# A transformer block with adaptive layer norm: the order of TensorE's products in the last row block's tail

## The chip, the cores and the metric

The kernel runs on one core of a Trainium2 chip. The metric is the device time of one execution in microseconds (us); the median of three runs is given.

## What is computed

The inputs are x (2048 rows of 576), weights for 32 heads of 18, a feed-forward layer of 4608, and a condition c. All is float32.

```python
mod = (_silu(c) @ w_mod).reshape(c.shape[0], 6, 1, -1)
sa, ca, ga, sb, cb, gb = (mod[:, i] for i in range(6))
h = _layernorm(x, axis=-1) * (1 + ca) + sa
x = x + ga * _A_ref(h, A_wqkv, A_wo)      # softmax attention, 32 heads, then @ wo
h = _layernorm(x, axis=-1) * (1 + cb) + sb
x = x + gb * _B_ref(h, B_w1, B_w2)        # silu(h @ w1) @ w2
```

## The kernel before, in words

The 2048 rows are worked on in four row blocks b = 0 to 3 of 512 rows, each of four tiles j of 128 rows. Every factor of a product outside attention is split into a high and a low float32r part, and a product is done as three (high x high, high x low, low x high); PASS lists these for the five contraction tiles kt, 14 steps in all (kt 4 has 64 rows and carries its low part in the other 64).

While attention of block b runs, the program fills TensorE's free slots with work of block b - 1. ORDER is the hand-written order of that mix; a planner (Plan, Filler) keeps dates for it. TensorE's order is the order in which the program emits its instructions; the order of ACT, DVE, GpSimd and of SyncE's DMA queue is found by a scheduler, which issues what is ready in its own simulated time. When attention of block 3 is over, `post(3)` runs with `last` true, and everything left is emitted in one row: the tail. Its stages, in TensorE's order, with lines:

1. Left work of block 2, the last second-layer group (weight tiles 32 to 35): a list `left` of 32 items, each of 3 products of 128x288. An item belongs to a row tile j and a half g of the 576 columns; `mlp2` (L1251) makes 12 products per bank, two banks per j. When a j is done, two adds (`add_x1`, L1103) put it on x1[j], and L1268 sends x1[j] out. `rest(n)` takes the next n items; REST = (16, 8, 0, 0) takes 16 before projection 0 and 8 before projection 1, and the last eight come after projection 3, two ahead of each step of its layer norm.
2. Out-projection `proj(j)` (L1084): 28 products of 128x288 for each j, 14 per bank. It needs the attention output as th and tl, made by `o_T` (L1077 to L1082) from the tile ou, which the last head group's DMAs (L1014) fill. Its adds need x1[j] of block 3, loaded by `prefetch(3)` at L1052. There are five x1 buffers for all blocks (`bufs=5`), and four tiles per block.
3. Layer norm of tile j (`ln_stat`, `ln_rs`, `ln_c`, L1112 to L1137), on DVE with one power on GpSimd; for j = 0 to 2 beside the next projection. The result is ob.
4. `h_T(kt)` (L1141): for each kt four transposes (one per j) into one bank, then ACT scales the bank into eq (`mod_out`, L472), DVE rounds eq to hh (`mod_hi`, L478), and DVE or GpSimd takes hl = eq - hh (`mod_lo`, L482, L484).
5. First layer `mlp1(i)` (L1218): a pair of weight tiles, 14 products of 128x512 for the first bank, then 14 for the second; then SiLU on ACT and DVE (L1244 to L1248) gives g tiles. Second layer as in 1, in groups of four g tiles, each group behind the next first-layer pairs; only the last group follows its own pair at once. w1 loads (L739, four buffers, which the wo tiles have before) and w2 loads (five buffers) wait for the products that free a buffer.

In a pair of banks the steps run 0 to 2n - 1, the first n for the first bank (class Pair, L531). `bank` (L1209) chooses the PSUM banks: psA has three, psF and psB two each, psV one. In the tail the first layer uses psA; second layer and transposes use psF and psB in turn, but block 2's left work only psF.

Of the kernel before, what the change touches and what calls it, by code (L numbers as in the profile page):

```python
# [9 lines left out]
F32 = mybir.dt.float32  # L10
# [8 lines left out]
P = 128  # L19
# [6 lines left out]
KT = 5  # L26
# [30 lines left out]
END = -4  # L57
END0 = 40
LP0 = 1000
REST = (16, 8, 0, 0)  # L60
LP = 8000
PB = 9
ORDER = (
# [43 lines left out]
GR = [[range(i, min(i + GS, n)) for i in range(0, n, GS)] for n in (28, 27)]  # L107
NG = len(GR[0])
GQ = (range(0, 5), range(5, 10), range(10, 14))
G2 = [range(i, i + 3) for i in range(0, 24, 3)]  # L110
GP = [range(i, i + 2) for i in range(0, 28, 2)]
MMC = 228
MMH = 131

# [292 lines left out]
def tile_adaln_block(ctx: ExitStack, tc: tile.TileContext, x, wqkv, wo, w1, w2, c, ccol, wfirst, wcol, out):  # L407
# [63 lines left out]
    def mod_out(ps, kt, which, tmp):  # L471
        nc.scalar.activation(tmp, ps, AF.Identity, scale=modc[:, 2 * which + 1, kt:kt + 1], bias=modc[:, 2 * which, kt:kt + 1])  # L472

    def mod_hi_ps(kt, hi_dst, ps):
        nc.vector.tensor_scalar(hi_dst, ps, modc[:, 1, kt:kt + 1], modc[:, 0, kt:kt + 1], op0=ALU.mult, op1=ALU.add)

    def mod_hi(hi_dst, tmp):
        nc.vector.tensor_copy(hi_dst, tmp)  # L478
# [52 lines left out]
    class Pair:  # L531
# [3 lines left out]

        def __init__(self, ps, ops, n, halves, planned=True, short=False):
            self.ps, self.ops, self.n, self.halves, self.planned = ps, ops, n, halves, planned
            self.end = 2 * n - 1 - (halves and short)  # L540
            self.both = halves and short
            if planned:
                self.release = [plan.take("f") for _ in ps]

        def step(self, s):
            late, i = divmod(s, self.n)
            if not self.halves:
                lhsT, rhs = self.ops(late, i)
                mm(self.ps[late], lhsT=lhsT, rhs=rhs, start=(i == 0), stop=(i == self.n - 1))  # L549
                return  # L550
            for h in (1, 0) if late else (0, 1):
                g = 1 - h if late else h
                lhsT, rhs = self.ops(g, self.n if self.both and s == self.n - 1 else i)
                rows = slice(64 * h, 64 * h + 64)
                done = mm(self.ps[g], lhsT=lhsT[rows], rhs=rhs[rows], start=(s == 0), stop=(s == self.end))  # L555
                if h == 1 and s == self.n - 1:
                    self.last = done
                    if self.planned:
                        self.change()
                        half["at"] = None  # L560
                        plan.op("A", plan.t + 200, 20, lambda t: half.update(at=t + TR))
                elif h == 1 and s == self.n:
                    tc.add_manual_dep(done.ins, self.turn.ins.name, SYNC, reason="the other halves' writes to this bank")
# [490 lines left out]
    def post(b):  # L1054
# [29 lines left out]
        def proj(j, part):  # L1084
            if part == 0:
                def ops(g, i):
                    kt, a, w = PASS[i]
                    return (c["tl"] if a else c["th"])[:, kt, j * P:(j + 1) * P], c["wo", kt][:, 1 - w, g * HH:(g + 1) * HH]

                settle(*[("wo", kt) for kt in range(KT)])  # L1090
                c["pp"] = Pair([bank("psp", psA)[:, :HH] for _ in range(2)], ops, 14, not state["tail"])
            for s in GP[part]:
                c["pp"].step(s)
            if part == len(GP) - 1:
                state["ln"] = b == 0
                c["x", j] = Event(plan)
                for g in range(2):
                    add_x1(j, g, c["pp"].ps[g], c["pp"].release[g], c["x", j].set)
# [39 lines left out]
        def ln_steps(j):  # L1138
            return [lambda: ln_stat(j, 0), lambda: ln_stat(j, 1), lambda: ln_rs(j), lambda: ln_c(j)]

        def h_T(kt):  # L1141
            if kt == 0:
                c["hh"] = pool.tile([P, KT, QB], F32R, tag="th", name="hh")
                c["hl"] = pool.tile([P, 4, QB], F32R, tag="tl", name="hl")
            ps = bank("psT", psF)
            c["hT", kt] = None
            chain([("A", 780), ("V", 800), ("G", 1290 if kt < 4 else 1900)], plan.t, plan.take("f"), lambda at: c.update({("hT", kt): at + 100}))
            for j in range(NST):
                nc.tensor.transpose(ps[:, j * P:(j + 1) * P], c["ob"][:, j, kt * P:(kt + 1) * P], ident)
            tmp, hi = etmp(), c["hh"][:, kt, :]  # L1150
            mod_out(ps, kt, 1, tmp)
            mod_hi(hi, tmp)
            if kt == 4 and not last:
                c["h2"] = const.tile([P, D], F32R, tag="ga", name="h2")[:, :QB]
                nc.gpsimd.tensor_copy(c["h2"], tmp)
            mod_lo(kt, hi, c["hl"][:, kt, :] if kt < 4 else None, tmp, nc.vector if last and kt % 2 == 0 else nc.gpsimd)

        def rest(n):
            for _ in range(min(n, len(left))):
                fl.add(*left.pop(0))  # L1160
# [7 lines left out]
            return all_ready(pair_need(), *[c.get(("th_at", kt)) for kt in range(KT)], weights_need(*[("wo", kt) for kt in range(KT)]) if b == 0 else 0)  # L1168

        for j in range(NST):  # L1170
            rest(REST[j])
            steps_ = dict(zip((1, 4, 8, 11), ln_steps(j - 1))) if j else {}
            for part in range(len(GP)):
                fl.add(MMH * len(GP[part]), lambda j=j, part=part: proj(j, part), need={0: pair_need if j else o_need, len(GP) // 2: half_need}.get(part))
                if b == 0 and j == 0 and part in (1, 4, 7, 10):
                    fl.add(0, lambda i=part // 3: w2_load(i))
                if part in steps_:
                    fl.add(0, steps_[part])
        for step in ln_steps(3):
# [1 line left out]
                fl.add(700)  # L1181
            rest(2)
            fl.add(0, step)
        rest(99)
        if b == 0 and not EARLY:
            fl.add(LP)

# [21 lines left out]
        def bank(name, pool_):  # L1209
            if last and pool_ is psA:  # L1210
                return psA.tile([P, 512], F32, tag="a", name=name)
            if last and state["tail2"]:
                state["tail2"] = False
                return psB.tile([P, 512], F32, tag="b", name=name, bufs=2)
            state["tail2"] = True
            return psF.tile([P, 512], F32, tag="f", name=name)

        def mlp1(i, part):  # L1218
            if part == 0:
                def ops(g, k):  # L1220
                    if k == 14:
                        return c["w1", i + g][:, 0, 4 * P:], c["h2"]
                    kt, a, w = PASS[k]
                    return c["w1", i + g][:, 1 - w, kt * P:(kt + 1) * P], (c["hl"] if a else c["hh"])[:, kt, :]

                settle(("w1", i), ("w1", i + 1))
                c["p1"] = Pair([bank("ps1", psA) for _ in range(2)], ops, 14, not state["tail"], short=not last)
            for s in GR[not last][part]:
                c["p1"].step(s)
            if part < NG - 1:  # L1230
# [17 lines left out]
                (nc.vector if last else nc.gpsimd).tensor_tensor(g[:, 1, :], t, f(g[:, 0, :]), op=ALU.subtract)  # L1248
                c["g", i + g_] = g

        def mlp2(i0, j, part):  # L1251
            if part == 0:
                def ops(g, n):
                    a, w = ((0, 0), (0, 1), (1, 0))[n % 3]
                    return c["g", i0 + n // 3][:, a, j * P:(j + 1) * P], c["w2", i0 + n // 3][:, 1 - w, g * HH:(g + 1) * HH]

                settle(*[("w2", i0 + n) for n in range(CH)])
                c["p2"] = Pair([bank("ps2", psF)[:, :HH] for _ in range(2)], ops, 3 * CH, not state["tail"])
            for s in G2[part]:
                c["p2"].step(s)  # L1260
            if part < len(G2) - 1:
                return
            if j == NST - 1:
                c["freed"] = i0 + 2 * CH - 1
            for hf in range(2):
                add_x1(j, hf, c["p2"].ps[hf], None if state["tail"] else c["p2"].release[hf])
            if i0 + CH == NFT:
                nc.sync.dma_start(out[b * QB + j * P:b * QB + (j + 1) * P, :], c["x1"][j])  # L1268

# [7 lines left out]
            fl.add(0, lambda i=i: w_load(i))  # L1277
        if b:
            fl.add(0, lambda: w2_load(0))
        if EARLY:  # L1280
            if b == 0:
                fl.add(LP)
            for kt in range(KT):
                fl.add(440, lambda kt=kt: h_T(kt), name=["h_T"], need=hT_need, mode="full")
                if b == 0 and kt > 2:
                    fl.add(0, lambda i=kt - 1: w_load(i))
# [14 lines left out]
                fl.add(MMC * len(GR[not last][part]), lambda part=part: mlp1(i, part), need={0: first_need, NG // 2: half_need}.get(part))  # L1301
                w_at(part, *loads)

        def add_mlp2(i0, add, *loads):
            def first_need():
                return all_ready(pair_need(), weights_need(*[("w2", i0 + n) for n in range(CH)]) if b == 0 else 0)

            for j in range(NST):
                for part in range(len(G2)):
                    add(MMH * len(G2[part]), lambda j=j, part=part: mlp2(i0, j, part), None, {0: first_need, len(G2) // 2: half_need}.get(part))  # L1310
                    w_at(j * len(G2) + part, *loads)

        add_mlp1(0, *([] if b else [(9, w_load, 4), (11, w_load, 5)]))
        for i0 in range(0, NFT, CH):
# [9 lines left out]
            else:  # L1324
                add_mlp1(i0 + 2, *([(0, w2_load, i0 + 1), (2, w2_load, i0 + 2), (4, w2_load, i0 + 3)] if b else []))
        if last:
            add_mlp2(NFT - CH, fl.add)
        else:
            fl.add(0, lambda: prefetch(b + 1))
            add_mlp2(NFT - CH, lambda *a: left.append(a))  # L1330

            def left_need():
                return all_ready(pair_need(), *c["gs"], weights_need(*[("w2", NFT - CH + n) for n in range(CH)])) if len(c["gs"]) == 2 else None
# [509 lines left out]
```

## Time and profile before

| | us |
|---|---|
| median of three runs (2340.99 to 2346.88) | 2342.13 |
| the profiled execution | 2339.21 |
| its span, first to last instruction | 2337.4 |
| TensorE busy | 2289.3 |
| DVE busy | 1762.3 |
| ACT busy | 1472.8 |
| GpSimd busy | 706.4 |
| mean granted TensorE clock | 0.992 of full |

The chain that ended last has 89% of the span on TensorE. In it the tail begins near 2062 us; the end is at 2337.4. PE is TensorE, POOL GpSimd, SP SyncE. A timeline row has start, length, engine, line, operation, tiles, how many instructions it merges, and in brackets the idle time before it and what ended that. A merged row's length runs from the first start to the last end, and the end of a product lies some 0.3 us behind its start, so rows overlap; products follow each other by their starts.

### The profile page before, as it was taken

The page shows a single profiled execution, that of the slowest core. Times are in us where ns is not written, and L with a number is a line of the kernel's source. Part 1 is how long each engine was busy: PE and PEld are TensorE (multiplying, and loading weights), DVE is VectorE, ACT ScalarE, POOL GpSimd, SP SyncE. Part 2 cuts the span into 40 slices and gives each one's busy share as a digit, 9 for nine tenths or more (in the row PEclk, how much of TensorE's full clock was granted, in tenths as well). Part 3 has the DMA queues.
Part 4 walks back from the last instruction along what each step waited for, and adds up shares of the span by engine and source line. Part 5 has one row for each costly group of instructions (what it writes and reads, how often), then busy time and mean ns, then how long its engine had stood idle before and what let it go on. Part 6 is the DMA issues. An engine that isn't in the chain of part 4 may idle for free.

```text
span 2337.4 us, 52323 instructions
## 1 busy us (share of the span) xinstructions
PE 2289.3 (98%) x19954; PEld 1581.3 (68%) x19954; DVE 1762.3 (75%) x3080; ACT 1472.8 (63%) x2712; POOL 706.4 (30%) x856
## 2 busy tenths in 40 slices
PE   7999999999899999999999999999999999999999
PEld 6974444444576776776677677777677767678998
DVE  7788899987788888877888888778887777343333
ACT  4347777776577777766677777666776677732221
POOL 4213333315556666664211111112211111110000
PEclk9999999998899999999999999999999999999999
DMA  7555555446556666765655545464644654345653
GB/s 277 175 175 177 180 186 175 157 150 197 187 187 222 216 217 210 233 216 202 217 171 169 187 169 166 161 198 156 205 161 161 205 180 172 110 164 193 220 199 115
DMA packets 201619, 433.55 MB, mean 185 GB/s; under 512 B 31506, under 2 KB 67762, under 8 KB 201370
## 3 DMA queue, kind: packets, MB, share of 16 engines
q1 hardware_dynamic: 201370, 430.21, 55.4%
q8 instruction: 159, 2.61, 0.5%
q14 instruction: 90, 0.74, 0.1%
HBM read 339.07 MB, written 86.33 MB: 182 GB/s over the span
## 4 chain that ended last, share of the span: by engine, by line
PE 89%; DVE 5%; DMA 2%; ACT 2%; POOL 1%; issue 1%; SPq 0%; DVEq 0%; ACTq 0%; POOLq 0%
PE ps L555 27%; PE psv L986 19%; PE psa L897 14%; PE ps L549 10%; PE psb L949 9%; PE psqk L661 3%; DVE mx L899 2%; PE psv L555 2%; PE psp L555 1%; PE psqk L555 1%; PE psv L1529 1%; DMA raw<-in_w 1%; PE psp L549 1%; PE psqk L1529 1%; DMA qt<-qscr 1%
## 5 line engine op out<-in xcount | busy, mean ns | idle before, releaser
L899 DVE TENSOR_REDUCE mx<-psa 128x1 f32<-128x512 f32 x2048 | 1328.9, 684 | 281.1 <-PE psb L949 166.6
L951 ACT ACTIVATE pt<-psb 128x512 f32<-128x512 f32 x2048 | 1148.5, 599 | 470.3 <-PE psb L949 301.1
L949 PE MATMUL psb<-qt,kb 56*128 56x512 f32 x2048 | 743.6, 421 | 3.5 <-ACT pt L951 3.5
L897 PE MATMUL psa<-ka,qt 54*128 54x512 f32 x2016 | 732.7, 417 | 10.9 <-DVE mx L899 8.8
L897 PEld LDWEIGHTS psa<-ka,qt 54*128 54x128 f32 x2016 | 347.5, 186 | 304.2 <-DVE mx L899 170.5
L986 PE MATMUL psv<-pt,vt 128*32 128x512 f32 x4096 | 512.6, 607 | 0.3 <-ACT ov L990 0.3
L555 PE MATMUL ps<-w2t,g 64*128 64x288 f32 x4992 | 412.4, 293 | 1.9 <-POOL w2t L782 1.2
L555 PEld LDWEIGHTS ps<-w2t,g 64*128 64x128 f32 x4992 | 384.6, 185 | 42.6 <-DVE x L1103 6.0
L949 PEld LDWEIGHTS psb<-qt,kb 56*128 56x128 f32 x2048 | 351.5, 186 | 27.8 <-ACT pt L951 17.1
L555 PE MATMUL ps<-hh,w1t 64*128 64x512 f32 x1944 | 352.3, 394 | 0.0
L1248 POOL TENSOR_TENSOR g<-etmp,g 128x512 fp32r<-128x512 f32 x108 | 137.5, 1293 | 387.2 <-ACT g L1247 336.9
L986 PEld LDWEIGHTS psv<-pt,vt 128*32 128x32 f32 x4096 | 102.5, 109 | 212.8 <-issue 205.1
L555 PEld LDWEIGHTS ps<-hh,w1t 64*128 64x128 f32 x1944 | 194.5, 186 | 43.3 <-POOL raw L778 3.4
L1110 POOL TENSOR_TENSOR x<-x,gt 128x288 f32<-128x288 f32 x116 | 93.3, 804 | 387.0 <-ACT gt L1109 382.2
L555 PE MATMUL ps<-hl,w1t 64*128 64x512 f32 x864 | 177.6, 391 | 0.0
L1103 DVE TENSOR_TENSOR x<-ps,x 128x288 f32<-128x288 f32 x184 | 83.2, 452 | 106.4 <-PE ps L549 71.6
L549 PE MATMUL ps<-w2t,g 128*128 128x288 f32 x960 | 130.8, 296 | 2.9 <-POOL g L1248 1.4
L549 PEld LDWEIGHTS ps<-w2t,g 128*128 128x128 f32 x960 | 128.6, 188 | 5.6 <-POOL g L1248 1.9
L1244 ACT ACTIVATE eq<-ps 128x512 f32<-128x512 f32 x36 | 21.6, 600 | 146.3 <-PE ps L549 146.3
L549 PE MATMUL ps<-hh,w1t 128*128 128x512 f32 x360 | 106.9, 390 | 0.5 <-DVE hh L484 0.5
L555 PEld LDWEIGHTS ps<-hl,w1t 64*128 64x128 f32 x864 | 88.6, 186 | 15.1
L1245 DVE SCALAR_TENSOR_TENSOR etmp<-etmp 128x512 f32<-128x512 f32 x108 | 74.4, 728 | 11.8 <-ACT etmp L1244 10.5
(157 smaller groups left out, 2122.8 us busy)
## 6 DMA issues: line engine op xcount, KB each, us to landing
w1t<-w1s SPq DMA_DIRECT2D x108, 640.0 KB
w2t<-w2s SPq DMA_DIRECT2D x108, 576.0 KB
kb<-kscr SPq DMA_DIRECT2D x512, 108.0 KB
ka<-kscr SPq DMA_DIRECT2D x504, 108.0 KB
w1s<-w1t SPq DMA_DIRECT2D x36, 640.0 KB
w2s<-w2t SPq DMA_DIRECT2D x36, 576.0 KB
vt<-vscr SPq DMA_DIRECT2D x32, 608.0 KB
qt<-qscr SPq DMA_DIRECT2D x128, 108.0 KB
```

Source lines behind the costliest of these rows:

```text
L549: mm(self.ps[late], lhsT=lhsT, rhs=rhs, start=(i == 0), stop=(i == self.n - 1))
L555: done = mm(self.ps[g], lhsT=lhsT[rows], rhs=rhs[rows], start=(s == 0), stop=(s == self.end))
L661: mm(qk_ps[0], lhsT=w[b][:, kt, :], rhs=(hTl if a else hTh)[:, kt, n * 512:(n + 1) * 512], start=(i == 0), stop=(i == 13))
L897: mm(ps, lhsT=t["q"][64 * j:64 * j + 54, hp, stt * P:(stt + 1) * P], rhs=t["a" if ("a", kc, hp) in t else "b", kc, hp][64 * j:64 * j + 54, ...
L899: return lambda: nc.vector.tensor_reduce(t["mx"][:, 2 * j + hp, stt, kc:kc + 1], ps, axis=AX.X, op=ALU.max)
L949: state["pe"] = mm(ps, lhsT=t["b", kt // 4, hp][64 * e:64 * e + 56, kt % 4 * P:(kt % 4 + 1) * P], rhs=t["q"][64 * e:64 * e + 56, hp, :], s ...
L951: nc.scalar.activation(t["P"][kt, hp][:, e, :], ps, AF.Exp, scale=SCALE)
L986: mm(t["ps"][32 * h:32 * h + 32, :], lhsT=t["v"][:, c0:c0 + 32], rhs=t["P"][kt, h // 2][:, h % 2, :], start=(kt == 0), stop=(kt == NKT - 1 ...
L1103: nc.vector.tensor_add(c["x1"][j][:, hs], ps, c["x1"][j][:, hs])
L1110: nc.gpsimd.tensor_add(c["x1"][j][:, hs], c["x1"][j][:, hs], t)
L1245: nc.vector.scalar_tensor_tensor(t, t, 1.0, u, op0=ALU.add, op1=ALU.mult)
L1248: (nc.vector if last else nc.gpsimd).tensor_tensor(g[:, 1, :], t, f(g[:, 0, :]), op=ALU.subtract)
```

## The change

- The left work of block 2 and the last group of block 3 go in the order THIRDS: for j = 0 and 1 together, over four banks, weight tiles 0 and 1 first, then tile 2, then tile 3; j = 2 and 3 as before. Block 2's left work in the tail may use psB too.
- LREST = (22, 0, 0, 0): 22 left items before projection 0; eight behind projection 3 as before; the last two behind the transposes.
- Projection 0 takes the products of kt 4 last, for both banks (LATE).
- h_T is done in two rounds: first the transposes of row tiles 0 to 2 for all five kt, into five banks (two psA, psV, two of psF and psB), then the fourth tile's, each followed by its scaling.
- In the last block hh is made by DVE from the PSUM bank (`mod_hi_ps`, a scale and a shift) instead of from eq.
- The first pair of the first layer goes kt by kt over both banks (BYKT).

```diff
-REST = (16, 8, 0, 0)
+REST, LREST = (16, 8, 0, 0), (22, 0, 0, 0)
...
-G2 = [range(i, i + 3) for i in range(0, 24, 3)]
+LATE = [12 * g + i for g in range(2) for i in range(12)]
+LATE = [s + 2 * (s >= 12) for s in LATE] + [12, 13, 26, 27]
+BYKT = [14 * g + i for a, b in ((0, 3), (3, 6), (6, 9), (9, 12), (12, 14)) for g in range(2) for i in range(a, b)]
+THIRDS = [(j, 12 * g + 3 * n) for part in ((0, 1), (2,), (3,)) for j in range(2) for g in range(2) for n in part] + [(j, 3 * n) for j in range(2, 4) for n in range(8)]
...
-    def mod_hi_ps(kt, hi_dst, ps):
-        nc.vector.tensor_scalar(hi_dst, ps, modc[:, 1, kt:kt + 1], modc[:, 0, kt:kt + 1], op0=ALU.mult, op1=ALU.add)
+    def mod_hi_ps(kt, hi_dst, ps, which=0):
+        nc.vector.tensor_scalar(hi_dst, ps, modc[:, 2 * which + 1, kt:kt + 1], modc[:, 2 * which, kt:kt + 1], op0=ALU.mult, op1=ALU.add)
...
         def step(self, s):
+            if not self.halves and self.order:
+                s = self.order[s]
...
-                c["pp"] = Pair([bank("psp", psA)[:, :HH] for _ in range(2)], ops, 14, not state["tail"])
+                c["pp"] = Pair([bank("psp", psA)[:, :HH] for _ in range(2)], ops, 14, not state["tail"], order=None if j else LATE)
...
-        def h_T(kt):
-            if kt == 0:
+        def h_T(kt, some=None):
+            if kt == 0 and some != 1:
...
-            ps = bank("psT", psF)
+            if some != 1:
+                if last and kt == 3:
+                    c["psT", kt] = psV.tile([P, QB], F32, tag="v", name="psT")
+                else:
+                    c["psT", kt] = bank("psT", psA if last and kt in (0, 4) else psF)
+            ps = c["psT", kt]
+            for j in range(NST) if some is None else range(NST - 1) if some == 0 else (NST - 1,):
+                nc.tensor.transpose(ps[:, j * P:(j + 1) * P], c["ob"][:, j, kt * P:(kt + 1) * P], ident)
+            if some == 0:
+                return
...
-            for j in range(NST):
-                nc.tensor.transpose(ps[:, j * P:(j + 1) * P], c["ob"][:, j, kt * P:(kt + 1) * P], ident)
             tmp, hi = etmp(), c["hh"][:, kt, :]
             mod_out(ps, kt, 1, tmp)
-            mod_hi(hi, tmp)
+            if last:
+                mod_hi_ps(kt, hi, ps, 1)
+            else:
+                mod_hi(hi, tmp)
...
-            rest(REST[j])
+            rest((REST if not last else LREST)[j])
...
-        rest(99)
+        if not last:
+            rest(99)
...
-            if last and state["tail2"]:
+            if state["tail"] and state["tail2"]:
...
-                c["p1"] = Pair([bank("ps1", psA) for _ in range(2)], ops, 14, not state["tail"], short=not last)
+                c["p1"] = Pair([bank("ps1", psA) for _ in range(2)], ops, 14, not state["tail"], short=not last, order=None if i else BYKT)
...
-        def mlp2(i0, j, part):
-            if part == 0:
+        def mlp2(i0, j, s0):
+            if ("p2", j) not in c:
...
-                c["p2"] = Pair([bank("ps2", psF)[:, :HH] for _ in range(2)], ops, 3 * CH, not state["tail"])
-            for s in G2[part]:
-                c["p2"].step(s)
-            if part < len(G2) - 1:
+                c["p2", j] = Pair([bank("ps2", psF)[:, :HH] for _ in range(2)], ops, 3 * CH, not state["tail"]), []
+            pair, steps = c["p2", j]
+            for s in range(s0, s0 + 3):
+                pair.step(s)
+                steps.append(s)
+            if len(steps) < 6 * CH:
                 return
+            del c["p2", j]
...
-        if EARLY:
+        if last:
+            for some in range(2):
+                for kt in range(KT):
+                    fl.add(330 if some == 0 else 110, lambda kt=kt, some=some: h_T(kt, some), mode="full")
+            rest(99)
+        elif EARLY:
...
-            for j in range(NST):
-                for part in range(len(G2)):
-                    add(MMH * len(G2[part]), lambda j=j, part=part: mlp2(i0, j, part), None, {0: first_need, len(G2) // 2: half_need}.get(part))
-                    w_at(j * len(G2) + part, *loads)
+            for j, s in THIRDS if late else [(j, s) for j in range(NST) for s in range(0, 6 * CH, 3)]:
+                add(MMH * 3, lambda j=j, s=s: mlp2(i0, j, s), None, None if late else {0: first_need, 3 * CH: half_need}.get(s))
+                w_at(j * 8 + s // 3, *loads)
...
-            add_mlp2(NFT - CH, fl.add)
+            add_mlp2(NFT - CH, fl.add, late=True)
...
-            add_mlp2(NFT - CH, lambda *a: left.append(a))
+            add_mlp2(NFT - CH, lambda *a: left.append(a), late=b == NQB - 2)
```

## Rows read from the trace of the kernel before

**Rows 1.** The page, part 1: busy time, share of the span, instructions.

```profile
PE 2289.3 (98%) x19954; PEld 1581.3 (68%) x19954; DVE 1762.3 (75%) x3080; ACT 1472.8 (63%) x2712; POOL 706.4 (30%) x856
```

**Rows 2.** Stretches: length, busy PE, PEld, DVE, ACT, POOL; clock, DMA share, GB/s.

```profile
2094.00:2106.00 12.00, 9.09 (x55) 7.01 (x54) 8.80 (x20) 3.64 (x5) 3.69 (x5) 1.00 1.00 396
2106.00:2150.00 44.00, 44.00 (x243) 38.98 (x242) 17.36 (x29) 12.32 (x20) 0.00 (x0) 1.00 0.61 215
...
1629.00:1650.00 21.00, 19.24 (x164) 9.60 (x163) 18.34 (x36) 12.98 (x23) 9.88 (x10) 1.00 0.95 340
```

**Rows 3.** Timeline of PE, from the tail's start to the first pair's end.

```profile
2065.19 1.06 PE L549 MATMUL ps<-w2t,g 128*128 128x288 f32 x6
...
2069.17 5.17 PE L549 MATMUL ps<-w2t,g 128*128 128x288 f32 x37 [0.56 <-POOL g L1248]
2074.18 0.42 PE L549 MATMUL psp<-wo,th 128*128 128x288 f32 x2
...
2076.92 0.80 PE L549 MATMUL psp<-wo,th 128*128 128x288 f32 x4 [1.00 <-DVE th L1082]
...
2093.48 3.35 PE L549 MATMUL ps<-w2t,g 128*128 128x288 f32 x24
...
2098.25 2.08 PE L1149 MATMUL psT<-ident,ob 128*128 128x128 f32 x17 [1.09 <-DVE ob L468]
...
2108.99 1.07 PE L549 MATMUL ps<-hh,w1t 128*128 128x512 f32 x4
```

**Rows 4.** The chain of waits: start, length, what (projections 1 to 3).

```profile
2082.51 11.13 PE psp L549 x84
```

**Rows 5.** Timeline of PE at the end: the last second-layer group.

```profile
2319.41 1.36 PE L549 MATMUL ps<-w2t,g 128*128 128x288 f32 x9
...
2322.43 11.54 PE L549 MATMUL ps<-w2t,g 128*128 128x288 f32 x85 [0.20 <-DVE g L1248]
```

**Rows 6.** Timeline of SyncE's DMA issues in the tail.

```profile
2083.03 0.34 SPq L1268 DMA_DIRECT2D out<-x  x1
2085.14 0.33 SPq L1052 DMA_DIRECT2D x<-in_x  x1
2092.21 2.13 SPq L739 DMA_DIRECT2D w1t<-w1s  x4
2094.44 3.44 SPq L739 DMA_DIRECT2D w2t<-w2s  x5
```

**Rows 7.** Timeline of SyncE's DMA issues at the head of block 2.

```profile
1640.95 0.33 SPq L1268 DMA_DIRECT2D out<-x  x1
...
1650.43 0.36 SPq L1052 DMA_DIRECT2D x<-in_x  x1
```

**Rows 8.** Groups by line and shape, 2062 to 2110: busy us, mean ns, idle before.

```profile
L1116 DVE BATCH_NORM_STATS2 st<-x 128x6 f32<-128x288 f32 x8 | 3.7, 460 | 0.2
L468 DVE TENSOR_SCALAR ob<-x,mv,rs 128x576 f32<-128x576 f32 x4 | 2.3, 576 | 0.1
L454 POOL TENSOR_TENSOR r<-ve,mhalf 128x1 f32<-128x1 f32 x4 | 2.2, 551 | 12.3 <-DVE ve L452 12.3
```

**Rows 9.** Timelines of DVE (the start, then the tail's h_T) and ACT (h_T).

```profile
41.30 0.81 DVE L475 TENSOR_SCALAR hTh<-psT,modc 128x512 fp32r<-128x512 f32 x1 [0.44 <-ACT etmp L472]
...
2099.43 0.43 DVE L478 CAST hh<-eq 128x512 fp32r<-128x512 f32 x1 [1.23 <-ACT eq L472]
2099.89 0.69 DVE L482 TENSOR_TENSOR hl<-eq,hh 128x512 fp32r<-128x512 f32 x1
...
2098.62 2.86 ACT L472 ACTIVATE eq<-psT,modc 128x512 f32<-128x512 f32 x4 [22.47 <-PE psT L1149]
```

**Rows 10.** Stretches, columns as in rows 2: TensorE nearly idle, then at work.

```profile
610.00:614.00 4.00, 0.68 (x7) 0.31 (x3) 2.47 (x5) 0.00 (x0) 2.60 (x4) 0.83 0.76 232
614.00:619.00 5.00, 4.81 (x19) 3.58 (x21) 2.07 (x6) 3.11 (x4) 1.34 (x4) 0.50 0.84 328
619.00:623.00 4.00, 2.69 (x16) 0.75 (x12) 2.82 (x6) 1.82 (x4) 4.00 (x4) 0.93 0.32 103
```

More of the change, by code (lines that the diff above doesn't have):

```diff
@@ L531, in tile_adaln_block, with __init__ @@
     class Pair:
-        def __init__(self, ps, ops, n, halves, planned=True, short=False):
-            self.ps, self.ops, self.n, self.halves, self.planned = ps, ops, n, halves, planned
+        def __init__(self, ps, ops, n, halves, planned=True, short=False, order=None):
+            self.ps, self.ops, self.n, self.halves, self.planned, self.order = ps, ops, n, halves, planned, order
             self.end = 2 * n - 1 - (halves and short)
@@ L1265, in mlp2 @@
             for hf in range(2):
-                add_x1(j, hf, c["p2"].ps[hf], None if state["tail"] else c["p2"].release[hf])
+                add_x1(j, hf, pair.ps[hf], None if state["tail"] else pair.release[hf])
             if i0 + CH == NFT:
@@ L1302, in add_mlp1, with add_mlp2 @@
                 w_at(part, *loads)
-        def add_mlp2(i0, add, *loads):
+        def add_mlp2(i0, add, *loads, late=False):
             def first_need():
                 return all_ready(pair_need(), weights_need(*[("w2", i0 + n) for n in range(CH)]) if b == 0 else 0)
-            for j in range(NST):
-                for part in range(len(G2)):
-                    add(MMH * len(G2[part]), lambda j=j, part=part: mlp2(i0, j, part), None, {0: first_need, len(G2) // 2: half_need}.get(part))
-                    w_at(j * len(G2) + part, *loads)
+            for j, s in THIRDS if late else [(j, s) for j in range(NST) for s in range(0, 6 * CH, 3)]:
+                add(MMH * 3, lambda j=j, s=s: mlp2(i0, j, s), None, None if late else {0: first_need, 3 * CH: half_need}.get(s))
+                w_at(j * 8 + s // 3, *loads)
         add_mlp1(0, *([] if b else [(9, w_load, 4), (11, w_load, 5)]))
```

## The prediction

> **What bounds the kernel now.** The page comes first: TensorE is busy 98% of the span [rows 1], so only its gaps can be won. The stages of the tail come next: from 2106 us on it is busy without a break (44.00 of 44.00 us), while in 2094 to 2106 it has 9.09 of 12.00 us and the DMA engines are full, at 396 GB/s [rows 2]. The stretches that follow are pure product work, so what the head of the tail saves or loses stays in the end time. Then TensorE's timeline, for where the gaps lie. Left products of block 2: 48 products of 288 columns start at 2065.19 and the first out-projection product at 2074.18 [rows 3]. A product of that width starts every 11.13 / 84 = 0.1325 us [rows 4], or 0.134 in the last run (85 in 11.54 us [rows 5]); 48 need 6.43 us and take 8.99, so 2.56 us are lost, on the last two g tiles of block 2. The projection's kt 4 products wait for th until 2076.92, where 12 products from 2074.18 would have ended at 2075.79: 1.13 us lost. After the projection (first left product 2093.48) the transposes wait for the fourth normalised tile (2098.25), and the first layer's first pair runs in pieces; of its 28 products of 512 columns (0.227 us each) the last start near 2109.2, so it ends at 2109.44 [rows 3]. At the end 96 products take from 2319.41 to 2333.97 [rows 5], 14.56 us where 13.0 are needed: 1.56 lost on the last two g tiles.
>
> **The change, part by part.** (a) Block 2's left products by weight tile over four banks. The third tile is first used after 24 products (2068.4), the fourth after 36 (2070.0); the fourth was complete at 2069.17 [rows 3]. All 2.56 us go. The banks are free: the first add ends well before item 17 wants its bank.
>
> (b) kt 4 last in projection 0, behind 66 left products instead of 48: 2065.19 + 66 x 0.134 = 2074.03, and 24 products more make 2077.2, later than 2076.92 [rows 3]. The 1.13 us go.
>
> The projection then runs through: it ends at P = 2065.19 + 8.84 + 112 x 0.1325 = 2088.87 instead of 2093.48, 4.6 us earlier (0.8 of it six products moved behind, paid back in (d)).
>
> (c) What the moved products carry. This decides. Item 24 of the left work ends tile j=2 of block 2; its last adds release an out transfer, and block 3's fourth x1 tile has the buffer of that tile (five buffers, four per block). SyncE shows the tie: out at 2083.03, the x load at 2085.14 as soon as it has landed [rows 6]. Before, item 24 stood ahead of projection 1. With 22 items ahead, items 23 and 24 come **after projection 3**, whose adds need that x1 tile. So the out transfer can issue only at P + 0.8 (six products) + 0.2 + 0.46 (add) = P + 1.5, and by then SyncE has issued four w1t loads (the first at 2092.21, P - 1.27, as projection 3 gives up its buffers) and one w2t (2094.44, P + 0.96) [rows 6]. Price, lower bound: 2.1 us for the out transfer and as much for the load of the same 288 KB, as with idle engines [rows 6]: x1 at P + 5.7. Upper bound: both stand behind all that was issued earlier: four w1t of 640 KB, three w2t of 576 KB, out and x, 4.98 MB. At 396 GB/s [rows 2] from P - 1.27 with 1.4 us of fixed time (2.1 less 0.73 of data) that is P + 12.7. The head of block 2 shows the same queue: an out issued at 1640.95, and the x load that waits for it only at 1650.43 [rows 7], with the engines 95% busy at 340 GB/s there [rows 2]; that pace gives P + 14.8. I take the middle of the two paces, P + 13.8, far from the lower bound, since rows 7 are the nearest case: x1 lands at 2102.7. The normalisation then needs two adds and two statistics (each some 0.46, on 128x288), r on GpSimd (0.55), ob (0.58) [rows 8] and six small operations, together 1.0, with a dozen hand-overs of some 0.035, an estimate: 4.4 us. The fourth tile stands at 2107.2, against 2098.2 before. The three-tile transposes end early and cover nothing of this; kt 4's even need a bank that projection 3's first add must free.
>
> (d) From the fourth tile to the end of the first pair: 11.2 us before (2098.25 to 2109.44) [rows 3]. Floor: five transposes at 0.11, six left products (0.8) and 28 x 0.227, 7.7 us. Ceiling: 11.2 + 0.8 and what DVE gets longer: hi from PSUM takes 0.81 us instead of 0.43, five times, 1.9 us [rows 9]: 13.9. And hi gains no overlap with ACT: on the start's transposes the same DVE operation stands idle for 0.44 us until ACT has read that bank [rows 9]. The Trainium skill says the same of two readers (PSUM — Partial Sum Buffer, PSUM bank collisions raise a hardware error); by a reading with overlap (d) would be 0.4 us less. Chained by hand (ACT 0.72 per kt, hi 0.8, lo 0.69 on DVE and about twice that on GpSimd, three eq buffers) the kt 4 parts are ready 8.2 us after the fourth tile, and with each kt used for both banks the pair ends at 9.6, near the middle of floor and ceiling. But TensorE has stood nearly still since 2093.5, over 10 us; after a stretch with 0.68 of 4 us busy the granted clock was at half, 1.2 GHz, for the next 5 us of work [rows 10]. Five us at half speed put TensorE's own end at 10.4 us, and I take that: 2107.2 + 10.4 = 2117.6, which is 8.2 later than 2109.44.
>
> (e) The last second layer by weight tile: 24 products before the third tile is read, and its g tiles are complete 3.0 us after 2319.41 [rows 5]; the last is first read 4.8 us after. Saved 1.56. The four adds of j = 0 and 1 bunch up, but the next pair needs its second bank only 1.6 us after its first. w1t 4 and 5 load after the whole pair, with idle DMA engines and 6 us before their use: nothing.
>
> Sum: +8.2 - 1.6 = **+6.6 us**. The profiled execution took 2339.2, so 2345.8; the median of the runs shown stands 2.9 above it, so 2348.7.
>
> **The rivals.** *The x1 tile is there in time*, so that the cover works. The fourth tile would stand at 2093.6 (P + 4.7), 24 products and 15 transposes take as long, and the pair ends 9.6 to 9.8 later, 2103.3: -6.1 - 1.6 = -7.7, 2334.4. For it: all the gaps of rows 3 and 5 are real. Against it: the buffers, as above. Chance 0.09; in it the change doesn't pay its DMA.
>
> *The transfers are served side by side*, or SyncE issues out ahead of the loads. Then x1 lands between P + 5.7 and P + 10; at the first, the fourth tile is at 2099.0, the pair ends at 2108.7, and the sum is -2.3 (2339.8); halfway it is about 2342. The Trainium skill has such a rule (DMA: Bandwidth & Descriptors, Issuing engines are not separate DMA queues): transfers run on the same 16 engines and interleave. Rows 7, where the x load had to wait 9.5 us for an out, speak against it for transfers of one issuer. Chance 0.12.
>
> *Slower: the clock.* Place: the first pair. If the half clock holds for the whole pair, 28 products take twice 6.36 us and it ends near 15.4 us after the fourth tile, 5 us later than I take: 2353.7. It decides from about 6 us at half speed on, since each us beyond 5 costs 0.5. For it: the still stretch here is three times that of rows 10. Against it: in rows 10 the next stretch is back at 0.93. Chance 0.09.
>
> **How the numbers follow.** The forecast's case has 0.70. A measurement tells about 0.3%, 7.0 us, from no change. Its own spread is P + 12.7 to P + 14.8 and about 1 us of (d): +4.5 to +8.6, nearly halved by 7.0: 0.37 within, 0.33 slower. With the rivals: faster 0.09, same 0.37 + 0.12 = 0.49, slower 0.33 + 0.09 = 0.42. The range leaves out most of the fast rival and the last of the clock's: 2340 to 2353.
>
> **What would show it.** Right: no TensorE gap in 2065 to 2089; the fourth x load of block 3 issued some 10 us after the end of projection 3; a TensorE gap of near 10 us in front of kt 4's transposes or the fourth tile's, with a granted clock under 1 behind it; DVE L475 after ACT L472 in the last block; no gap at the last g tiles. Wrong: transposes of the fourth tile within 6 us of the last projection product.

## The result, and the profile after

The changed kernel's median is 2344.84 us (22 runs), that of the kernel before in the same comparison 2339.17 us (22 runs; the three shown ahead had 2342.13). The ratio is 1.0024, with a 95% interval of 1.0016 to 1.0032: about 5.7 us slower, within the 0.3% that the prediction called no change, and 0.9 us from the +6.6 of its sum. The profiled execution has a span of 2342.8 us, 5.4 more than before's. One of the five runs of left_24, further down, is a slow one of 12309 us, which counts in that kernel's median and not in its ratio.

TensorE does the same work as in [rows 1] in nearly the same busy time (2288.0 us, before 2289.3); the loss is all gap.

Page, part 1, of the changed kernel:

```profile
PE 2288.0 (98%) x19954; PEld 1581.4 (67%) x19954; DVE 1764.1 (75%) x3080; ACT 1472.2 (63%) x2712; POOL 707.8 (30%) x856
```

TensorE's timeline in the changed kernel answers to [rows 3] and, with its last row, to [rows 5]. In this kernel L554 is the line of all products, L1157 that of the transposes.

```profile
2064.79 9.02 PE L554 MATMUL ps<-w2t,g 128*128 128x288 f32 x66
...
2088.50 3.35 PE L554 MATMUL ps<-w2t,g 128*128 128x288 f32 x24
2091.68 1.47 PE L1157 MATMUL psT<-ident,ob 128*128 128x128 f32 x12
2103.13 0.88 PE L1157 MATMUL psT<-ident,ob 128*128 128x128 f32 x3 [9.98 <-DVE x L1108]
2106.58 1.33 PE L1157 MATMUL psT<-ident,ob 128*128 128x128 f32 x5 [2.58 <-DVE ob L471]
2107.56 1.79 PE L554 MATMUL ps<-w2t,g 128*128 128x288 f32 x6
...
2115.62 1.52 PE L554 MATMUL ps<-hh,w1t 128*128 128x512 f32 x6
...
2326.50 12.88 PE L554 MATMUL ps<-w2t,g 128*128 128x288 f32 x96
```

Read it as two wins and one loss. The 66 left products run without a break (before, 48 took 8.99 us), the projection ends at P = 2088.50, 23.71 us after the tail's start instead of 28.29, and the last 96 products have no gap. In between TensorE stands for 9.98 us in front of the last three of the early transposes and for 2.58 us in front of the fourth tile's. Four of the six products of the last-but-one row belong to the first pair, so it ends at 2115.62 + 4 x 0.227 = 2116.53. From the first left product to there it is 51.7 us, before 44.25.

The chain of waits of the changed kernel, in that stretch, says what it stood for (start, length, what):

```profile
2089.49 0.47 DVE x L1108
...
2089.98 8.93 DMA out<-x
...
2098.97 3.48 DMA x<-in_x
...
2102.53 0.82 DVE x L1108 x2
...
2105.95 0.59 DVE ob L471
```

SyncE's issues in the changed kernel, the answer to [rows 6], with L1287 as the line of out and L1057 that of x:

```profile
2087.22 2.07 SPq L744 DMA_DIRECT2D w1t<-w1s  x4
2089.34 0.47 SPq L744 DMA_DIRECT2D w2t<-w2s  x1
2089.98 0.71 SPq L1287 DMA_DIRECT2D out<-x  x1
2091.48 0.87 SPq L744 DMA_DIRECT2D w2t<-w2s  x2
2098.97 0.33 SPq L1057 DMA_DIRECT2D x<-in_x  x1
```

The out transfer is issued 1.48 us after P, behind five weight loads, and takes 8.93 us where 2.1 were enough in [rows 6]; only then can the load of block 3's fourth x1 tile be issued, and it takes 3.48. The tile is there at 2102.45, P + 13.95.

Stretches of the changed kernel, columns as in [rows 2]:

```profile
2093.00:2098.00 5.00, 0.15 (x2) 0.00 (x0) 0.00 (x0) 0.00 (x0) 0.00 (x0) 0.93 0.99 354
2098.00:2107.00 9.00, 1.29 (x5) 0.92 (x6) 3.12 (x11) 0.00 (x0) 0.78 (x2) 0.50 0.41 167
2107.00:2111.00 4.00, 4.00 (x15) 3.30 (x14) 3.09 (x5) 2.90 (x4) 1.48 (x1) 0.50 0.35 120
2111.00:2117.00 6.00, 6.00 (x28) 4.91 (x28) 3.38 (x6) 1.46 (x3) 1.47 (x2) 1.00 0.50 170
```

While TensorE stands the DMA engines are full (0.99), and the clock falls to half; it is full again from 2111 on, after some four us of work.

### The profile page after: what moved, and what is told of

Same layout as the page of the kernel before. It is cut to its first block, busy times and chain, and to the rows that moved or that the text cites. A ratio compares the mean times of both kernels' runs of the same rounds, so it can differ in the third digit from the quotient of the medians.

```text
span 2342.8 us, 52324 instructions
## 1 busy us (share of the span) xinstructions
PE 2288.0 (98%) x19954; PEld 1581.4 (67%) x19954; DVE 1764.1 (75%) x3080; ACT 1472.2 (63%) x2712; POOL 707.8 (30%) x856
## 4 chain that ended last, share of the span: by engine, by line
PE 89%; DVE 4%; DMA 3%; ACT 1%; POOL 1%; issue 1%; SPq 0%; DVEq 0%; ACTq 0%; POOLq 0%
PE ps L560 27%; PE psv L991 19%; PE psa L902 14%; PE ps L554 10%; PE psb L954 9%; PE psqk L666 3%; DVE mx L904 2%; PE psv L560 1%; PE psp L560 1%; PE psqk L560 1%; PE psv L1552 1%; PE psp L554 1%; DMA ka<-kscr 1%; DMA raw<-in_w 1%; PE psqk L1552 1%
## 5 line engine op out<-in xcount | busy, mean ns | idle before, releaser
L554 PE MATMUL ps<-w2t,g 128*128 128x288 f32 x960 | 130.2, 296 | 0.0
L554 PEld LDWEIGHTS ps<-w2t,g 128*128 128x128 f32 x960 | 129.1, 189 | 1.5 <-issue 0.8
L554 PE MATMUL ps<-hh,w1t 128*128 128x512 f32 x360 | 107.1, 391 | 0.0
L1261 DVE SCALAR_TENSOR_TENSOR etmp<-etmp 128x512 f32<-128x512 f32 x108 | 75.8, 742 | 11.8 <-ACT etmp L1260 10.9
```

Source lines behind the costliest of these rows:

```text
L1261: nc.vector.scalar_tensor_tensor(t, t, 1.0, u, op0=ALU.add, op1=ALU.mult)
```

## The experiments

The theory: the two moved items hold block 2's third row tile in its buffer, so that a store and a load, both behind the weight loads, come into the path. Its rivals: the gap is the price of the new order itself (transposes, hi from PSUM, the pair's order), or the issue order of one engine rather than the load of all queues sets it.

Timing tells some 3 us here, less than some parts are worth, so beside the timing each kernel's tail is read from its profile: from the first left product to the end of the span (272.2 us before, 278.0 after), and from P to the end of the first pair.

| kernel | median us | ratio, interval | first left product | P | end of pair | P to pair | tail |
|---|---|---|---|---|---|---|---|
| changed | 2344.84 | 1.0024, 1.0016 to 1.0032 | 2064.79 | 2088.50 | 2116.53 | 28.0 | 278.0 |
| x_own_buffer | 2330.02 | 0.9953, 0.994 to 0.9966 | 2067.98 | 2091.70 | 2106.22 | 14.5 | 264.5 |
| left_24 | 2329.77 | 0.9949, 0.9935 to 0.9962 | 2059.73 | 2084.23 | 2098.42 | 14.2 | 265.0 |
| before_two_moved | 2354.68 | 1.0059, 1.0045 to 1.0073 | 2063.59 | 2091.10 | 2123.77 | 32.7 | 288.2 |
| out_on_act | 2344.35 | 1.0018, 1.0008 to 1.0027 | 2062.30 | 2086.01 | 2114.11 | 28.1 | 278.1 |
| loads_behind_x | 2337.34 | 0.9996, 0.9986 to 1.0005 | 2061.99 | 2085.70 | 2105.71 | 20.0 | 270.0 |
| left_24_one_round | 2332.04 | 0.9965, 0.9953 to 0.9977 | 2065.31 | 2089.81 | 2103.94 | 14.1 | 265.0 |
| left_24_hi_from_sbuf | 2330.37 | 0.996, 0.9948 to 0.9972 | 2062.31 | 2086.82 | 2100.45 | 13.6 | 264.5 |
| left_24_bank_by_bank | 2333.08 | 0.9974, 0.9963 to 0.9984 | 2059.97 | 2084.47 | 2100.67 | 16.2 | 267.0 |
| x_own_hi_from_sbuf | 2331.13 | 0.9964, 0.9951 to 0.9976 | 2063.95 | 2087.66 | 2101.66 | 14.0 | 264.1 |
| end_only | 2336.41 | 0.9989, 0.9979 to 1.0 | 2061.46 | | | | 270.6 |

P to pair is 16.0 us before. Ratios are against runs of the kernel before on the same chip (medians 2340.89, 2339.58 and 2339.06 in the three groups of runs); a ratio is estimated from all the runs and need not be that of the two medians.

**x_own_buffer.** The change, with a buffer outside the five for block 3's fourth x1 tile (the one tagged ga among the constants); nothing else differs.

```diff
-c["x1"].append(pool.tile([P, D], F32, name="x1", bufs=5))
+c["x1"].append(const.tile([P, D], F32, tag="ga", name="x1") if b == NQB - 1 and j == 3 else pool.tile([P, D], F32, name="x1", bufs=5))
```

> The change as it is, but block 3's fourth x1 tile takes another buffer, free since block 2's first layer ended, so that it waits for no out transfer. Theory (the late x1 tile): the x load goes before the projections; the fourth normalised tile stands about 4.7 us after the last projection product instead of 18; no TensorE gap over 1 us there; the granted clock stays at full; 7.7 us less than before (6 to 9 less), 12 to 14 less than the change. Rival (the loss lies in the two rounds of transposes, DVE reading PSUM and the first pair over two banks): the time stays within 1.5 us of the change's, 4 to 7 above before.

TensorE's timeline of this kernel, from P to the last products of the pair:

```profile
2091.70 3.35 PE L554 MATMUL ps<-w2t,g 128*128 128x288 f32 x24
2094.88 2.35 PE L1157 MATMUL psT<-ident,ob 128*128 128x128 f32 x20
2096.98 1.04 PE L554 MATMUL ps<-w2t,g 128*128 128x288 f32 x6
2098.51 0.73 PE L554 MATMUL ps<-hh,w1t 128*128 128x512 f32 x2 [0.49 <-DVE hh L478]
2100.19 0.50 PE L554 MATMUL ps<-hl,w1t 128*128 128x512 f32 x1 [0.95 <-DVE hl L485]
...
2105.31 1.52 PE L554 MATMUL ps<-hh,w1t 128*128 128x512 f32 x6
```

All twenty transposes run in one piece: the gap is gone, the pair ends 13.5 us earlier after P, and the tail is 7.7 us shorter than before's, to the tenth what the prediction gave for its rival *the x1 tile is there in time*. The timing gives more, 10.9 us (8.0 to 14.0 by the interval), and more than the 6 to 9 expected; "What stays open" comes back to it. The out transfer stands behind the loads here too; nobody waits for it. So the buffer is the cause of the loss.

**left_24.** The six products of the two moved items go back ahead of projection 0, so that nothing of j = 2 is left behind projection 3.

```diff
-REST, LREST = (16, 8, 0, 0), (22, 0, 0, 0)
+REST, LREST = (16, 8, 0, 0), (24, 0, 0, 0)
```

> The change with 24 left items ahead of projection 0 instead of 22; the eight others come behind projection 3 and none behind the transposes. Theory (the late x1 tile): out of tile 2 and the x load go some 10 us before projection 3 ends, ahead of the weight loads; 6 to 8 us less than before, up to 1 us more than with a buffer of its own, since nothing covers the first scaling. Rival (the loss lies in the form of the transposes and the first pair): within 1.5 us of the change's time, 4 to 7 above before.

SyncE's issues in this kernel:

```profile
2072.15 0.38 SPq L1287 DMA_DIRECT2D out<-x  x1
2077.00 0.33 SPq L1057 DMA_DIRECT2D x<-in_x  x1
2082.95 2.06 SPq L744 DMA_DIRECT2D w1t<-w1s  x4
```

Store and load are issued before the weights, 5.95 us between the load and the first w1t. The tail is 265.0: one number in one line is worth 13 us of it (13.8 from P to the end of the pair).

**before_two_moved.** The reverse: the kernel before, with the same two items moved behind projection 3 and nothing else.

```diff
-REST = (16, 8, 0, 0)
+REST, LREST = (16, 8, 0, 0), (16, 6, 0, 0)
...
-            rest(REST[j])
+            rest((REST if not last else LREST)[j])
```

> The kernel before with one thing moved: the last two left items of row tile 2 (six products, two adds, one out transfer) from ahead of projection 1 to behind projection 3. Theory (the late x1 tile): the out stands behind four w1t loads and a w2t load, the x1 tile lands some 14 us after the projection's end and the fourth normalised tile stands 18 after it instead of 4.7; 11 to 14 us more than before, with the clock at half for part of it. Rival (six products moved cost nothing by themselves): within 1 us of before.

The chain of waits of this kernel:

```profile
2092.58 8.64 DMA out<-x
...
2101.29 7.00 DMA x<-in_x
...
2112.42 2.20 PE psT L1149 x9
```

TensorE's transposes of the fourth tile start only at 2112.42, and the move alone costs 13.8 us by timing and 16.0 in the tail: the loss needs none of the new order. The x load is slower than in the change, 7.00 us, with all four remaining w2t loads, not two, issued ahead of it (at 2094.08); x1 lands at P + 17.2, where 14 was expected.

**out_on_act.** The change, with that one out and that one x load issued by ACT, whose queue has no weight loads.

```diff
-nc.sync.dma_start(c["x1"][j], x[b * QB + j * P:b * QB + (j + 1) * P, :D])
+(nc.scalar if b == NQB - 1 and j == 3 else nc.sync).dma_start(c["x1"][j], x[b * QB + j * P:b * QB + (j + 1) * P, :D])
...
-nc.sync.dma_start(out[b * QB + j * P:b * QB + (j + 1) * P, :], c["x1"][j])
+(nc.scalar if b == NQB - 2 and j == 2 else nc.sync).dma_start(out[b * QB + j * P:b * QB + (j + 1) * P, :], c["x1"][j])
```

> The change, with the out transfer of block 2's row tile 2 and the load of block 3's fourth x1 tile issued by ACT instead of SyncE; the order of all else is the same. Theory A (transfers of one issuer are served in the order of issue, those of another issuer beside them): x1 lands 6 to 10 us after the projection's end instead of 14; 4 to 8 us less than the change, from 2 less to 2 more than before. Theory B (all transfers are served in the order of issue, whoever issues): the out still takes about 9 us and the time is the change's, 4 to 7 above before.

The queues of this kernel in 2080 to 2105 (packets, MB, share of 16 engines):

```profile
q1 hardware_dynamic: 1008, 4.39, 46.4%
q10 hardware_dynamic: 288, 0.59, 6.0%
```

and its chain of waits:

```profile
2087.49 7.83 DMA out<-x
...
2095.41 4.57 DMA x<-in_x
```

The two transfers do run on a queue of their own, q10, and it wins nothing: 7.83 + 4.57 = 12.40 us against 8.93 + 3.48 = 12.41, x1 again at P + 14.0, the tail the same. The Trainium skill says that each DMA engine takes turns, packet by packet, between the queues that have work (DMA: Bandwidth & Descriptors, Queues, rings and completion order). By even turns, out would have been through once about as many bytes of the loads had passed. The run does not show that, and the measurement decides: by 2095 the engines had moved 3.38 MB (307 GB/s in 2084 to 2095, the first load issued at 2084.73), and the five loads issued ahead of out have 3.51 MB together with it. Here transfers ended nearly in the order in which they were issued, whoever issued them. Why is not settled by this run.

**loads_behind_x.** The change, with the first weight loads of block 3 held until that x load has landed: the same transfers, in another order.

```diff
-            nc.sync.dma_start(f(make()), f(scr))
-            return
+            done = nc.sync.dma_start(f(make()), f(scr))
+            return state["tail"] and key[1] < 4 and tc.add_manual_dep(done.ins, state["x3"].ins.name, SYNC, reason="behind the last x tile")
...
-            nc.sync.dma_start(c["x1"][j], x[b * QB + j * P:b * QB + (j + 1) * P, :D])
+            state["x3"] = nc.sync.dma_start(c["x1"][j], x[b * QB + j * P:b * QB + (j + 1) * P, :D])
```

> The change, with the first four w1t and w2t loads of block 3 made to wait for block 3's fourth x1 tile, so that the out transfer and the x load meet idle DMA engines; TensorE's, DVE's, ACT's and GpSimd's orders are the same. Theory (most of the loss is the queue of weight loads ahead of the out transfer): x1 lands about 6.2 us after the end of projection 3 instead of 14, the fourth normalised tile stands 10.6 after it, the weights land in time; 6 to 8 us less than the change, 3 less to 1 more than before. Rival (the round trip of out and load costs as much without a queue, or the weight loads, now later, hold TensorE): within 2 us of the change, 4 to 6 above before.

The chain of waits of this kernel:

```profile
2087.18 2.10 DMA out<-x
...
2089.30 2.61 DMA x<-in_x
```

its PE timeline:

```profile
2088.88 1.47 PE L1157 MATMUL psT<-ident,ob 128*128 128x128 f32 x12
2092.63 0.60 PE L1157 MATMUL psT<-ident,ob 128*128 128x128 f32 x3 [2.27 <-DVE x L1108]
2096.07 1.33 PE L1157 MATMUL psT<-ident,ob 128*128 128x128 f32 x5 [2.84 <-DVE ob L471]
...
2099.58 0.58 PE L554 MATMUL ps<-hl,w1t 128*128 128x512 f32 x1
```

and three stretches of it, columns as in [rows 2]:

```profile
2090.50:2093.00 2.50, 0.37 (x3) 0.31 (x3) 0.98 (x3) 0.00 (x0) 0.00 (x0) 0.98 0.39 117
2093.00:2096.00 3.00, 0.23 (x2) 0.00 (x0) 2.13 (x9) 0.00 (x0) 0.55 (x1) 0.50 0.94 358
2096.00:2100.00 4.00, 3.93 (x15) 3.28 (x16) 2.62 (x5) 2.48 (x4) 1.23 (x2) 0.53 0.99 384
```

x1 lands at P + 6.2, near the lower bound that the prediction gave (P + 5.7), and the pair ends 8.0 us earlier than in the change. That splits the 13.5 us between the change and x_own_buffer: 8.0 are the weight loads ahead in the queue, 5.5 the bare way of the tile out and in again. The tail is 2.2 us shorter than before's, and the timing is level with before within its interval.

**left_24_one_round.** left_24 with each kt's four transposes together: without the two rounds.

```diff
-            for some in range(2):
+            for some in (None,):
-                    fl.add(330 if some == 0 else 110, lambda kt=kt, some=some: h_T(kt, some), mode="full")
+                    fl.add(440, lambda kt=kt, some=some: h_T(kt, some), mode="full")
```

> The change with 24 left items ahead, and the transposes in one round, four for each kt as before, all behind the fourth tile but three. Theory (after the fourth tile ACT and DVE set the pace, and the transposes of 0.1 us run ahead of them): the stage from the end of projection 3 to the end of the pair takes 14.2 to 14.8 us, against 14.2; no difference that the timing shows. Rival (the transposes moved beside the normalisation are worth their own time): 15 transposes, 1.6 us more.

Its PE timeline:

```profile
2092.99 0.49 PE L1157 MATMUL psT<-ident,ob 128*128 128x128 f32 x3
2094.57 2.08 PE L1157 MATMUL psT<-ident,ob 128*128 128x128 f32 x17 [1.09 <-DVE ob L471]
```

14.1 us from P to the end of the pair, 14.2 in left_24: the early transposes win nothing. TensorE waits 1.09 us before the fourth tile instead of 1.28 us for hh behind it. DVE's first hh starts 1.24 us after the fourth tile here (2095.75, ob done at 2094.51) and 1.23 there (2090.17, 2088.94): the scaling by ACT and the split on DVE set the pace in both.

**left_24_hi_from_sbuf** and **x_own_hi_from_sbuf.** left_24 and x_own_buffer with hh taken from eq as before, not from the PSUM bank.

```diff
-            if last:
+            if False:
                 mod_hi_ps(kt, hi, ps, 1)
```

> The change with 24 left items ahead, and hh made as before, by a DVE copy of eq in SBUF instead of from the PSUM bank. In the run with 24 items the stage from the end of projection 3 to the end of the first pair takes 14.2 us. Theory (DVE's list sets the end of the pair, and reading PSUM saves no wait): five operations of 0.43 instead of 0.81 us; the stage ends 0.5 to 1.5 us earlier, 12.7 to 13.7 us. Rival (reading the bank directly starts hh earlier): the stage is up to 1 us longer. Either is near the limit of the timing; the trace decides.

> The change with a buffer of its own for block 3's fourth x1 tile, and hh made by a DVE copy of eq as before. Theory (DVE's list sets the end of the first pair): the stage from the end of projection 3 to the end of the pair, 14.5 us with the buffer alone, takes 13.0 to 13.9 us; 8 to 10 us less than before, the least of all kernels here or level with 24 items and the same copy. Rival (the six products behind the transposes already cover it): 14.5 us, and the time of the buffer alone.

DVE's first hh in left_24_hi_from_sbuf:

```profile
2092.76 0.43 DVE L481 CAST hh<-eq 128x512 fp32r<-128x512 f32 x1 [1.23 <-ACT eq L475]
```

and the first two in the changed kernel, DVE:

```profile
2107.91 1.53 DVE L478 TENSOR_SCALAR hh<-psT,modc 128x512 fp32r<-128x512 f32 x2 [1.38 <-ACT eq L475]
```

Reading the bank is no earlier (both wait for ACT's eq) and takes longer: 0.80 us each in the groups of the changed kernel, instead of 0.43. The pair ends 0.6 us sooner in the one and 0.5 in the other without it; the timing can't tell that. In x_own_hi_from_sbuf the 14.0 us are just above the 13.0 to 13.9 expected.

**left_24_bank_by_bank.** left_24 with the first pair's products in the old order, 14 for one bank and 14 for the other.

```diff
-                c["p1"] = Pair([bank("ps1", psA) for _ in range(2)], ops, 14, not state["tail"], short=not last, order=None if i else BYKT)
+                c["p1"] = Pair([bank("ps1", psA) for _ in range(2)], ops, 14, not state["tail"], short=not last, order=None)
```

> The change with 24 left items ahead, and the first pair of the first layer in the old order, 14 products for one bank, then 14 for the other. Theory (the scaled parts of the kt come one by one over some 8 us, so that products of both banks for each kt fill the waits): the stage from the end of projection 3 to the end of the pair takes 15.5 to 17 us instead of 14.2, and 1.3 to 2.8 us more in all. Rival (TensorE waits only for the first kt): 14.2 us, no difference.

Its PE timeline in the pair:

```profile
2092.59 0.50 PE L554 MATMUL ps<-hl,w1t 128*128 128x512 f32 x1 [0.58 <-DVE hl L485]
...
2096.36 0.49 PE L554 MATMUL ps<-hl,w1t 128*128 128x512 f32 x1 [0.61 <-POOL hl L485]
```

16.2 us from P to the end of the pair: the order by kt is worth 2.0, since each split tile feeds both banks before the next is needed.

**end_only.** The kernel before, with the new order THIRDS in the last second-layer group alone; the left items, the projection, the transposes, hh and the first pair are as before. These are the lines of the edit that set the order:

```diff
-            add_mlp2(NFT - CH, fl.add)
+            add_mlp2(NFT - CH, fl.add, late=True)
...
-            add_mlp2(NFT - CH, lambda *a: left.append(a))
+            add_mlp2(NFT - CH, lambda *a: left.append(a), late=False)
```

> The kernel before with one part of the change: the last group of the last block in the new order over four banks. Theory: the 96 products run through, 12.9 us from the first start to the last end instead of 14.5; 1.6 us less than before (1 to 2). Rival (four banks and four adds at once hold TensorE up at row tile 2): a gap of 0.3 us or more at half of the group, and less than 1 us saved.

Its last products, on PE's timeline:

```profile
2315.70 12.88 PE L554 MATMUL ps<-w2t,g 128*128 128x288 f32 x96
```

The gaps of [rows 5] are gone, and the tail is 270.6: 1.6 less.

## Why the prediction was right

Times are counted from the tail's first left product or from P, as in the prediction's steps.

| step | predicted | measured |
|---|---|---|
| (a), (b): start of the tail to P | 23.68 us | 23.71 us |
| (c): out issued | P + 1.5 | P + 1.48 |
| (c): x1 landed | P + 13.8 | P + 13.95 |
| (c): normalisation | 4.4 | 4.1 |
| (d): fourth tile to end of the pair | 10.4 | 10.0 |
| (e): at the end | 1.56 less | 1.7 less |
| sum | +6.6 | +5.8 (tail), +5.7 (medians) |

By the prediction's own terms the sum is +6.5: x1 at 2102.7 and 4.4 us of normalisation put the fourth tile at 2107.1, not 2107.2. Its time, 2348.7 us, is 3.9 above the median measured: 3.0 of that is the base (2342.13 of three runs, 2339.17 of 22), 0.9 the sum.

- **(a), (b)** held: no gap in 66 left products nor in projection 0, and P 4.6 us earlier after the start.
- **(c)**, the step that decides, held in place, cause and size. x_own_buffer and left_24 take the loss away by two ways that share nothing but the buffer, before_two_moved makes it without the rest of the change. The size rests on the nearest case, the queue at the head of block 2 [rows 7], and not on the lower bound; loads_behind_x shows that the lower bound is near what the same two transfers cost with nothing ahead of them. That P + 13.8 is within 0.15 us is in part luck: it was the middle between two paces read elsewhere, 396 and 340 GB/s, which gave P + 12.7 and P + 14.8. In the change the engines, full from 2088.2 to 2101.6, moved at 366.
- **(d)** was 0.4 us too long, and that is its clock term. The prediction gave 9.6 by hand and put 0.8 on it for a clock at half. The clock was at half, as expected, until 2111, 4.5 us behind the fourth tile. In loads_behind_x it is at half until near 2100 (0.53 in 2096 to 2100), under 4 us behind the fourth tile; TensorE, though slow, waits for DVE there (0.6 us for the first hl, done at 2099.52, its product at 2099.58), and the pair ends 9.7 us after that tile (2096.02 to 2105.71), near the 9.6 by hand. In the change it ends 10.0 after it. That difference of 0.3 us is the most that these runs show of the term. A slow TensorE there fills time in which a fast one waits for hh and hl: 0.49 and 0.95 us, in the rows of x_own_buffer. That kernel does not price the term: at full clock (1.00 in 2096 to 2107) the stretch takes 10.2 us (2096.01 to 2106.22), but ACT scales the first bank 0.82 us after the fourth tile instead of 0.56, behind sixteen transposes in a row, and DVE does an add of 0.36 us between its first two hh.
- hi from PSUM **gains no overlap**, as (d) said; it costs 0.5 to 0.6. The Trainium skill's rule on two readers of a bank (PSUM — Partial Sum Buffer, PSUM bank collisions raise a hardware error) agrees with the trace: DVE's L478 starts after ACT's eq, having stood idle for 1.38 us.
- The rival *the x1 tile is there in time* was rightly priced at -7.7 (264.5 against 272.2) and rightly set aside. *Side by side* falls with x1 at P + 13.95, and for two issuers with out_on_act. *Slower: the clock* falls with the clock's full level from 2111 on.

What stays open: in two versions without the loss the timing lies below before's by more than the tail does (10.9 us against 7.7 in x_own_buffer, 11.1 against 7.2 in left_24). The tail doesn't show the rest, and no run here was made to find it. But all four kernels timed against the same 15 runs of before (median 2340.89) lie 2.2 to 3.9 us lower by timing than by tail, with the loss or without it (before_two_moved 13.8 against 16.0, out_on_act 3.5 against 5.9); in the other two groups it is between 1.6 lower and 0.5 higher (left_24_one_round 7.5 less against 7.2, x_own_hi_from_sbuf 7.9 against 8.1). That points at this group's runs of before, not at the versions, but it is not shown.

The six versions without the loss beat both kernels, at 0.9949 to 0.9974 of before. But for left_24_bank_by_bank their intervals overlap, so the timing picks none of the five; by the tail x_own_hi_from_sbuf is shortest, 264.1 us. The simplest is left_24.

## What to carry to other kernels

Before a group of products is moved, follow what its last result releases: here a store, by it a buffer, by that a load, and at the end the tile that the stage behind waits for. Price such a store and load by the transfers that will have been issued before them, not by their own bytes: 12.4 us in the queue, 4.7 with nothing ahead. And this stage, whose pace is set by ACT and DVE, won nothing from transposes made early on TensorE; an order in which each tile that they deliver is used twice won 2 us.

## What the runs showed that was not expected

- A second issuer was no way past the full queue: on q10 out needed 7.83 us behind five weight loads of q1, and store and load together took as long as on q1, 12.40 and 12.41 us.
- The clock fell to half in loads_behind_x though TensorE's gaps are only 2.27 and 2.84 us long: it is at 0.98 in 2090.5 to 2093 and at 0.50 in the next 3 us, with few transposes between the gaps.
- The half clock cost the first pair little: with 4.5 us of it behind the fourth tile the pair ended 10.0 us after that tile, with under 4 us of it 9.7, and TensorE waited for DVE even so.
